# Adding exp(-m) to the softmax denominators on TensorE, and taking a batch's token maxima later, in a fused attention and soft-MoE kernel

## The chip, the core and the metric

The kernel runs on one core of a Trainium2 chip. A core has a matrix engine (TensorE, PE in the profile; its weight loads are PEld), a vector engine (VectorE, DVE), a scalar engine (ScalarE, ACT), GpSimd (POOL) and SyncE (SP). Each works through its own instructions in order, and they wait for one another by semaphores. POOL and SP also issue DMAs here. PE writes to PSUM, which DVE and ACT read; POOL works in SBUF.

The metric is the device time of one launch in microseconds. Three runs of the kernel before took 297.56, 299.50 and 299.66 us; the median is 299.5.

## The reference

For each of 8 batches and 12 heads, with 448 tokens and 64 features per head, it computes attention with a softmax whose denominator has one more term, exp(-m):

```
scores = scale * q @ k.T
m = max(scores, -1);  e = exp(scores - m)
attn = e / (sum(e, -1) + exp(-m) + 1e-09)
out = attn @ v
```

The output, 3584 tokens by 768, goes into a soft mixture of experts with 8 experts of 4 slots each:

```
logits = x @ phi                            # 3584 x 32
d = softmax over tokens;   slot_input = d.T @ x
slot_out[e] = relu(slot_input[e] @ w1[e]) @ w2[e]
c = softmax over slots;    result = c @ slot_out
```

Both softmaxes subtract a maximum first: the one for c the maximum of each token (over the 32 slots), the one for d the maximum of each slot (over the tokens).

## The kernel before

**Pairs and slots.** Heads are taken in 48 pairs, six pairs to a batch. The main loop (L758) runs over slots s, one pair each, in two half-slots y = 0 and 1; the order of every engine's work is written out by hand. In its slot a pair has its transposed scores computed on PE (`Bk`: a score product, L367, and a product that subtracts the maximum, L370, both into ps_b buffers of a pool of four), then exponentials on ACT (L372, L402). Between these stand the score products of a later pair (`A`, L285, into ps_a buffers of a pool of three), whose row maxima DVE takes (L287; L307 for the last 64 tokens). PE also transposes q and k of the pair six slots ahead (`T`, L256; copied by ACT at L263 or by DVE at L265).

**Denominators.** The product of the exponentials with v (`AV`, L436) has a column of ones beside the 64 columns of v, so column 64 of each of its seven tiles of 65 columns is the sum of the exponentials. All seven lie in one PSUM bank, of which there is one. Key blocks i = 0 and 1 are multiplied in the pair's own slot, i = 2 and 3 in the first half of the next one, followed by the eight products of the last 64 queries. Then `N1` copies the bank into ubuf on ACT (L449), and `N2` adds exp(-m) and 1e-9 on DVE (L464), takes the reciprocal (L465) and scales on POOL (L469, L479, L480) into x. `PX` transposes x on PE (L501) and ACT casts it (L507).

**exp(-m).** Every third slot a group of three pairs has its maxima prepared: `W1` on POOL (L318, L314), `W2` on PE (L336, L337), `W3` on ACT: a cast (L342), and two exponentials (L345, L348) that write ec, three pairs by seven columns in f32. There are 17 groups.

**A batch's part of the experts.** The list `post` spreads a batch's steps over half-slots of the following pairs. The first makes the logits on PE (`l_mm`, L535, into ps_l), copies them to l in SBUF on ACT (`l_ev`, L558) and takes the token maxima on DVE (`c_max`, L562). Half a slot later PE transposes l (`l_turn`, L570, with the f32 identity identf) and DVE takes maxima over it (L572), and POOL subtracts the token maxima (`c_sub`, L577). `s_max` (L582, L583), `d_sub` (L591), the exponentials (L596, L601), `s_mm` (L623), `s_add` (L632) and `c_turn` (L627, L628) follow. The last batch has an order of its own. After the loop the experts and the result are computed.

POOL's queue also issues the loads of q, k, v and of the expert weights between its other work, SP's the weights staged in memory and the output.

Of the kernel before, what the change touches and what calls it, by code (L numbers as in the profile page):

```python
# [10 lines left out]
AX = mybir.AxisListType  # L11
AF = mybir.ActivationFunctionType
ALU = mybir.AluOpType
# [13 lines left out]
W65 = 65  # L27
# [4 lines left out]
def kernel(  # L32
# [10 lines left out]
    nc = tc.nc  # L43
    B, H, S, D = q.shape
# [5 lines left out]
    KC = DD // 128  # L50
# [3 lines left out]
    NPAIR = B * PB  # L54
# [14 lines left out]
    identf = const.tile([128, 128], F32, name="identf")  # L69
# [87 lines left out]
    with ExitStack() as at:  # L157
# [73 lines left out]
        mx, ngm, ec, mT, eT, av, us = {}, {}, {}, {}, {}, {}, {}  # L231
# [39 lines left out]
        group = {n: (m, n - a) for m, (a, z) in enumerate(zip(firsts, firsts[1:] + [NPAIR])) for n in range(a, z)}  # L271
        mg, mpl = (lambda n: group[n][0]), (lambda m: (0, (firsts + [NPAIR])[m + 1] - firsts[m]))
# [67 lines left out]
        def W3(g):  # L340
            t = psm.tile([128, S], BF16, tag="mT", name="mT")
            nc.scalar.copy(t, st["ps_m"][:, 0:S])  # L342
            mT[g] = t
            e = psm.tile([128, NP, 7], F32, tag="ec", name="ec", bufs=3)
            nc.scalar.activation(e[:, :, 0:6].rearrange("p l (i h) -> p i l h", i=3),  # L345
                                 ngm[g][:, 0:18].rearrange("p (i l h) -> p i l h", i=3, h=2),
                                 AF.Exp, scale=scale)
            nc.scalar.activation(e[:, :, 6], ngm[g][:, 18:21], AF.Exp, scale=scale)  # L348
            ec[g] = e


# [63 lines left out]
        def av_tile(n):  # L415

            if n >= NPAIR - 3:
                return psA.tile([128, 512], F32, tag="a", name="ps_av")
            return psV.tile([128, 512], F32, tag="v", name="ps_av")

        def AV(n, i, qs):
            g, pl = divmod(n, NP)
            if i == 0 and qs[0] == 0:
                av[n] = av_tile(n)
            a = av[n]
            if n == NPAIR - 1 and i == 0 and qs[0] == 3:
                av_half["ps"] = psA.tile([128, 512], F32, tag="a", name="ps_av")
            for u in qs:
                for hl in range(2):
                    if u < 3:  # L430
                        c0 = (2 * u + hl) * W65
                        o, qc = a[:, c0:c0 + W65], slice(u * 128, (u + 1) * 128)
                    else:
                        t, z = (av_half["ps"], 0) if n == NPAIR - 1 else (a, 6 * W65)
                        o, qc = t[64 - 64 * hl:128 - 64 * hl, z:z + W65], slice(384, 448)
                    nc.tensor.matmul(o, eT[n, i, hl][:, qc], vp[g % 2][:, 2 * pl + hl, i, 0:W65],  # L436
                                     start=(i == 0 and u == 0 and hl == 0) or (u == 3 and i == 0 and n == NPAIR - 1),
                                     stop=(i == 3), skip_group_check=True)

        av_half = {}  # L440
        on_pool = lambda n: n < NPAIR - 4
# [10 lines left out]
        def N2(n):  # L452
            g, pl = divmod(n, NP)
            b, pb = divmod(n, PB)
            u = us[n]
            eng = nc.gpsimd if on_pool(n) else nc.vector
            rec = psm.tile([128, 7], F32, tag="rec", name="rec", bufs=3)
            e = ec[mg(n)][:, group[n][1], :]
            if n == NPAIR - 1:
                nc.vector.scalar_tensor_tensor(rec[:, 6:7], av_half["ps"][:, D:W65], 1e-9, e[:, 6:7],  # L460
                                               op0=ALU.add, op1=ALU.add)
                nc.vector.scalar_tensor_tensor(rec[:, 0:6], u[:, 0:6, D], 1e-9, e[:, 0:6], op0=ALU.add, op1=ALU.add)
            else:
                nc.vector.scalar_tensor_tensor(rec, u[:, :, D], 1e-9, e, op0=ALU.add, op1=ALU.add)  # L464
            nc.vector.reciprocal(rec, rec)  # L465
            x = xb[b % 2]
            c = pb * 128
            rec2 = psm.tile([128, 2], F32, tag="rec2", name="rec2", bufs=3)
            eng.tensor_mul(  # L469
                x[:, 0:3, c:c + 128].rearrange("p i (h d) -> p i h d", h=2),  # L470
                u[:, 0:6, 0:D].rearrange("p (i h) d -> p i h d", h=2),
                rec[:, 0:6].rearrange("p (i h) -> p i h", h=2).unsqueeze(3).to_broadcast([128, 3, 2, D]))
            if n == NPAIR - 1:

                for h in range(2):
                    r = slice(64 - 64 * h, 128 - 64 * h)
                    nc.scalar.mul(x[r, 3, c + 64 * h:c + 64 * h + 64], av_half["ps"][r, 0:D], rec[r, 6:7])
                return
            eng.tensor_scalar(rec2, halfm, rec[:, 6:7], None, op0=ALU.mult)  # L479
            eng.tensor_mul(  # L480
                x[:, 3, c:c + 128].rearrange("p (h d) -> p h d", h=2),
                u[:, 6, 0:D].unsqueeze(1).to_broadcast([128, 2, D]),
                rec2.unsqueeze(2).to_broadcast([128, 2, D]))
# [32 lines left out]
        def P(b):  # L516
            l, new = lb[b % 2], lb[(b + 1) % 2][:, 4, :]
            eng = nc.gpsimd if b < B - 2 else nc.vector
            x = xb[b % 2]
            v = {}  # L520
# [3 lines left out]
            def l_mm(js):  # L524
                if js[0] == 0:
                    if b < B - 1:
                        v["ps_l"] = pa([128, 4, NS], F32, "ps_l")
                    else:
                        t = psV.tile([128, 512], F32, tag="v", name="ps_l")
                        v["ps_l"] = t[:, 0:4 * NS].rearrange("p (i s) -> p i s", i=4)  # L530
                        v["ps_lT"] = t[:, 4 * NS:4 * NS + 129]

                def plain(j, tiles=range(4)):
                    for i in tiles:
                        nc.tensor.matmul(v["ps_l"][:, i, :], xT(b, j)[:, i * 128:(i + 1) * 128], phi_sb[:, j, :],  # L535
                                         start=(j == 0 and i == 0), stop=(j == KC - 1), skip_group_check=True)

                for j in js:
                    if b < B - 1 or j == 0:
                        plain(j)  # L540
                    if b == B - 1 and j == 3:
                        nc.tensor.matmul(v["ps_lT"][:, 128:129], flat(old),
                                         ident[:, 0:1], start=False, stop=True, skip_group_check=True)
                    if b == B - 1:

                        for i in range(4):
                            nc.tensor.matmul(v["ps_lT"][NS * i:NS * i + NS, 0:128], phi_sb[:, j, :],
                                             xT(b, j)[:, i * 128:(i + 1) * 128],
                                             start=False, stop=(j == KC - 1), skip_group_check=True)
                        if j == KC - 1:  # L550
                            l_turn()
                            keep_busy(2)
                            s_max()
                        if j:
                            plain(j)
# [3 lines left out]

            def c_max():  # L560
                m = psm.tile([128, 4], F32, tag="cm", name="cm")
                nc.vector.reduce_max(m, v["ps_l"] if b < B - 1 else l[:, 0:4, :], axis=AX.X)  # L562
                v["cm"] = m

            def l_turn():
                if b == B - 1:
                    ps = v["ps_lT"]
                else:
                    ps = pa([128, 128], F32, "ps_lT")
                    nc.tensor.transpose(ps, flat(l[:, 0:4, :]), identf)  # L570
                m = psm.tile([128, 1], BF16, tag="sm", name="sm")
                nc.vector.reduce_max(m, ps, axis=AX.X)  # L572
                v["sm"] = m
                v["z"] = psm.tile([128, 9, NS], F32, tag="z", name="z", bufs=1)
# [75 lines left out]

            both = lambda *fs: (lambda: [f() for f in fs])
            if b < B - 1:
                return [both(lambda: l_mm(range(KC)), l_ev, c_max), both(l_turn, c_sub), both(s_max, d_sub),
                        both(exps, corr)] + ([c_turn, both(s_mm, s_add)] if late(b) else [both(s_mm, s_add), c_turn])
            return [lambda: l_mm([0]), lambda: l_mm([1]), lambda: l_mm([2]), lambda: l_mm([3]), lambda: l_mm([4]),
                    both(lambda: l_mm([PB - 1]), l_ev,
# [34 lines left out]
        ps = psV.tile([128, 512], F32, tag="v", name="ps_idle")  # L691
# [255 lines left out]
        for half in range(2):  # L947
            for bp in range(B // 2):
                o = (half * (B // 2) + bp) * 4
                nc.tensor.matmul(ps_cs[:, o:o + 4], cT[:, bp, half, :, :].rearrange("p b j -> p (b j)"), band,  # L950
                                 start=True, stop=True)
# [80 lines left out]
```

## Time and profile before

| what | value |
|---|---|
| median of 3 runs | 299.5 us |
| span of the profiled execution | 299.0 us |
| granted PE clock, mean | 0.956 (1.00 until 270 us) |
| main loop | about 33 to 250 us |
| busy in the stretch 120 to 140 us | PE 19.96, ACT 19.08, DVE 19.48, POOL 16.60 of 20 us |
| busy from 260 to 270 us | PE 9.71, DVE 3.82, ACT 4.02, POOL 0.00 of 10 us |

What lies around the span of the profiled execution is taken as the difference to the median, 0.5 us. In the rows below, a group of instructions has its line, engine, operation, output and inputs, shape and count, then busy time and the mean duration of one in ns, then the engine's idle time before them and what ended it. In an answer in order of time the columns are start and duration in us, engine, line, operation, tiles, shape and count; in brackets stands the idle time before it and what released it. A matmul's duration holds its passage through the array, and the next can start long before its end, so how fast PE goes is read from the starts. A row of a stretch has its length, then busy us and counts of PE, PEld, DVE, ACT and POOL, then granted clock, DMA share and GB/s.

### The profile page before, as it was taken

The numbers are of one execution on the slowest core, as the hardware profiler recorded it, in microseconds if no ns is written. First come the engines' busy times: TensorE is split into PE (matmuls) and PEld (weight loads), VectorE is DVE, ScalarE is ACT, GpSimd is POOL, SyncE is SP. The second block draws the span as 40 slices with busy tenths as digits, with TensorE's granted clock in tenths as the row PEclk, the third lists the DMA queues.
The fourth block names the chain that finished last, engine by engine and source line by source line (L and its number), as shares of the span: only waits on it lengthen the run. The fifth ranks groups of instructions, "written<-read, shape, count | busy, mean of one in ns | idle before, by whom it ended". The sixth has DMA issues, their size and how long they took to land.

```text
span 299.0 us, 12398 instructions
## 1 busy us (share of the span) xinstructions
PE 271.4 (91%) x5174; PEld 162.5 (54%) x5174; DVE 249.7 (84%) x581; ACT 249.8 (84%) x559; POOL 195.9 (66%) x391
## 2 busy tenths in 40 slices
PE   5999899999999999999899999999999999996820
PEld 4445456566666566566556666656665555652100
DVE  5899799999999989999889999998999675537930
ACT  3569999999899989998989899989999987337820
POOL 8792887979696979887879697978686633000000
PEclk9999999999999999999999999999999999997555
DMA  7999998999999999999999999999799989908997
GB/s 132 147 143 208 149 138 138 188 165 188 185 204 179 184 176 202 163 182 182 202 159 184 176 199 152 196 183 196 125 150 187 213 185 263 344 10 318 380 453 322
DMA packets 47015, 58.67 MB, mean 196 GB/s; under 512 B 2800, under 2 KB 39920, under 8 KB 46704
## 3 DMA queue, kind: packets, MB, share of 16 engines
q0 software_dynamic: 40304, 42.29, 89.6%
q1 hardware_dynamic: 6656, 15.60, 13.8%
q8 instruction: 40, 0.66, 0.8%
q14 instruction: 15, 0.12, 0.1%
HBM read 89.16 MB, written 15.14 MB: 349 GB/s over the span
## 4 chain that ended last, share of the span: by engine, by line
PE 68%; ACT 10%; DVE 6%; POOL 6%; issue 4%; DMA 2%; DVEq 0%; POOLq 0%; ACTq 0%
PE ps_av L436 15%; PE ps_a L285 10%; PE ps_b L367 7%; PE ps_b L370 7%; PE ps_t L256 5%; PE ps_b L396 5%; PE ps_x L501 3%; PE ps_b L399 3%; ACT W L402 2%; PE ps_o L925 2%; DVE mx L298 2%; PE ps_s L623 2%; PE ps_h L862 2%; PE ps_so L882 2%; ACT W L263 2%
## 5 line engine op out<-in xcount | busy, mean ns | idle before, releaser
L287 DVE TENSOR_REDUCE mx<-ps_a 128x1 f32<-128x448 f32 x250 | 137.3, 613 | 4.6 <-PE ps_a L285 3.5
L372 ACT ACTIVATE W<-ps_b 128x448 bf16<-128x448 f32 x250 | 120.4, 574 | 0.0
L285 PE MATMUL ps_a<-W 64*128 64x448 bf16 x250 | 80.9, 352 | 0.0
L367 PE MATMUL ps_b<-W 64*128 64x448 bf16 x250 | 70.5, 352 | 1.1
L436 PE MATMUL ps_av<-W 128*128 128x65 bf16 (+1 forms) x1536 | 64.9, 196 | 2.2 <-issue 1.6
L436 PEld LDWEIGHTS <-W 128*128 128x128 bf16 (+1 forms) x1536 | 50.5, 100 | 30.2 <-issue 26.4
L370 PE MATMUL ps_b<-mT,sel 64*128 64x448 bf16 x250 | 66.5, 350 | 0.0
L469 POOL TENSOR_TENSOR W<-ubuf,rec 128x384 bf16<-128x384 f32 x44 | 36.3, 824 | 35.7 <-ACT W L507 19.3
L402 ACT ACTIVATE W<-ps_b 128x448 bf16<-128x448 f32 x86 | 46.1, 574 | 2.0 <-PE ps_b L399 2.0
L256 PEld LDWEIGHTS <-W 64*64 64x64 bf16 x1344 | 29.3, 112 | 12.7 <-issue 4.3
L507 ACT CAST W<-ps_x 128x512 bf16<-128x512 f32 x47 | 28.6, 608 | 7.4 <-PE ps_x L501 7.2
L256 PE MATMUL ps_t<-ident,W 64*64 64x64 bf16 x1330 | 30.6, 195 | 2.4 <-ACT W L215 1.4
L307 DVE TENSOR_REDUCE mx<-ps_a 128x1 f32<-128x448 f32 x48 | 29.5, 615 | 1.4 <-PE ps_a L304 1.4
L285 PEld LDWEIGHTS <-W 64*128 64x128 bf16 x250 | 23.4, 94 | 9.8
L114 POOL DMA_DIRECT2D W<-in_moe_w_dram x30 | 22.6, 755 | 7.9 <-PE ps_b L399 7.8
L370 PEld LDWEIGHTS <-sel 64*128 64x128 bf16 x250 | 19.6, 94 | 14.4 <-issue 5.6
L396 PE MATMUL ps_b<-W 64*64 64x448 bf16 (+1 forms) x134 | 27.1, 374 | 0.3
L449 ACT COPY ubuf<-ps_av 128x455 f32<-128x455 f32 x44 | 25.1, 571 | 0.8 <-POOL W L408 0.6
L399 PE MATMUL ps_b<-mT,sel 64*64 64x448 bf16 (+1 forms) x134 | 25.1, 354 | 0.1
L263 ACT COPY W<-ps_t 128x896 bf16<-128x896 bf16 x21 | 19.5, 927 | 6.5 <-PE ps_t L256 6.5
L298 DVE TENSOR_REDUCE mx<-ps_a 128x1 f32<-128x448 f32 x38 | 21.1, 616 | 1.9 <-PE ps_a L294 1.9
L480 POOL TENSOR_TENSOR W<-ubuf,rec 128x128 bf16<-128x128 f32 x44 | 17.5, 398 | 3.7
(156 smaller groups left out, 446.6 us busy)
## 6 DMA issues: line engine op xcount, KB each, us to landing
W<-in_moe_w_dram POOLq DMA_DIRECT2D x24, 768.0 KB, 9.9
W<-in_v_dram POOLq DMA_DIRECT2D x32, 192.0 KB, 6.5
out_dram<-W SPq DMA_DIRECT2D x2, 2688.0 KB, 10.0
W<-in_q_dram POOLq DMA_DIRECT2D x15, 336.0 KB, 6.3
W<-in_k_dram POOLq DMA_DIRECT2D x15, 336.0 KB, 7.5
stage<-in_moe_w_dram POOLq DMA_DIRECT2D x4, 768.0 KB, 9.6
W<-stage SPq DMA_DIRECT2D x4, 576.0 KB, 7.3
out_dram<-W SPq DMA_DIRECT2D x6, 384.0 KB, 3.0
```

The costliest lines, as they stand in the source:

```text
L256: nc.tensor.transpose(o, src[r, pl, tok * D:(tok + 1) * D], ident[r, r])
L285: nc.tensor.matmul(ps[:, 0:S], t[r, 0, i * 128:(i + 1) * 128], t[r, 1, :], start=True, stop=True)
L287: nc.vector.reduce_max(m[:, c:c + 1], ps[:, 0:S], axis=AX.X)
L307: nc.vector.reduce_max(mx[g][:, c:c + 1], ps[:, 0:S], axis=AX.X)
L367: nc.tensor.matmul(pss[hl][:, 0:S], t[rs[hl], 1, cols], t[rs[hl], 0, :], start=True, stop=False)
L370: nc.tensor.matmul(pss[hl][:, 0:S], sel[rs[hl], 2 * pl + hl:2 * pl + hl + 1].to_broadcast([64, 128]), mT[mg(n)][rs[hl], :], start=False, s ...
L372: nc.scalar.activation(e[:, hl, :], pss[hl][:, 0:S], AF.Exp, scale=scale)
L396: nc.tensor.matmul(outs[hl], t[rs[hl], 1, cols], t[rs[hl], 0, :], start=True, stop=False)
L399: nc.tensor.matmul(outs[hl], sel[rs[hl], 2 * pl + hl:2 * pl + hl + 1].to_broadcast([64, m]), mT[mg(n)][rs[hl], :], start=False, stop=True)
L402: nc.scalar.activation(e, p[:, 0:S], AF.Exp, scale=scale)
L436: nc.tensor.matmul(o, eT[n, i, hl][:, qc], vp[g % 2][:, 2 * pl + hl, i, 0:W65], start=(i == 0 and u == 0 and hl == 0) or (u == 3 and i == ...
L469: eng.tensor_mul(x[:, 0:3, c:c + 128].rearrange("p i (h d) -> p i h d", h=2), u[:, 0:6, 0:D].rearrange("p (i h) d -> p i h d", h=2), rec[: ...
```

## The change

There are two edits.

The first moves the sum of the denominators to PE. POOL adds 1e-9 to ec once for each group. After the products of key block i = 3 PE multiplies the f32 identity by the seven f32 columns of the pair's ec and accumulates them onto column 64 of the seven tiles in PSUM. The copy in ubuf then holds the whole denominator, and DVE only takes the reciprocal. The last pair keeps its sums on DVE.

The second lets `c_max` of all batches but the last read the copy l in SBUF in place of ps_l, and issues it half a slot later, after the transposition of l and ahead of the maxima over it.

```diff
             nc.scalar.activation(e[:, :, 6], ngm[g][:, 18:21], AF.Exp, scale=scale)
+            nc.gpsimd.tensor_scalar(e, e, 1e-9, None, op0=ALU.add)
             ec[g] = e
...
+            if i == 3 and qs[0] == 0 and n < NPAIR - 1:
+
+                nc.tensor.matmul(a[:, 0:7 * W65].rearrange("p (s c) -> p s c", c=W65)[:, :, D], identf,
+                                 ec[mg(n)][:, group[n][1], :], start=False, stop=True, skip_group_check=True)
...
             if n == NPAIR - 1:
-                nc.vector.scalar_tensor_tensor(rec[:, 6:7], av_half["ps"][:, D:W65], 1e-9, e[:, 6:7],
-                                               op0=ALU.add, op1=ALU.add)
-                nc.vector.scalar_tensor_tensor(rec[:, 0:6], u[:, 0:6, D], 1e-9, e[:, 0:6], op0=ALU.add, op1=ALU.add)
-            else:
-                nc.vector.scalar_tensor_tensor(rec, u[:, :, D], 1e-9, e, op0=ALU.add, op1=ALU.add)
-            nc.vector.reciprocal(rec, rec)
+                nc.vector.tensor_add(rec[:, 6:7], av_half["ps"][:, D:W65], e[:, 6:7])
+                nc.vector.tensor_add(rec[:, 0:6], u[:, 0:6, D], e[:, 0:6])
+            nc.vector.reciprocal(rec, rec if n == NPAIR - 1 else u[:, :, D])
...
                 m = psm.tile([128, 4], F32, tag="cm", name="cm")
-                nc.vector.reduce_max(m, v["ps_l"] if b < B - 1 else l[:, 0:4, :], axis=AX.X)
+                nc.vector.reduce_max(m, l[:, 0:4, :], axis=AX.X)
                 v["cm"] = m
...
                     nc.tensor.transpose(ps, flat(l[:, 0:4, :]), identf)
+                    c_max()
                 m = psm.tile([128, 1], BF16, tag="sm", name="sm")
...
-                return [both(lambda: l_mm(range(KC)), l_ev, c_max), both(l_turn, c_sub), both(s_max, d_sub),
+                return [both(lambda: l_mm(range(KC)), l_ev), both(l_turn, c_sub), both(s_max, d_sub),
```

## The prediction

> **What bounds the kernel now.** I read the page's busy shares and chain first, then the busy times by stretch, the instructions in order of time on PE, DVE and ACT over two slots, and last the groups by line and shape.
>
> ```profile
> PE 271.4 (91%) x5174; PEld 162.5 (54%) x5174; DVE 249.7 (84%) x581; ACT 249.8 (84%) x559; POOL 195.9 (66%) x391
> ...
> PE 68%; ACT 10%; DVE 6%; POOL 6%; issue 4%; DMA 2%; DVEq 0%; POOLq 0%; ACTq 0%
> ```
>
> The chain is mostly PE, but that share hides short stalls, because a matmul's recorded time is longer than its step in the stream. The stretch of one batch (six slots, one pair of heads each) says more:
>
> ```profile
> 90.43:120.05 29.62, 28.85 (x593) 18.20 (x592) 27.81 (x66) 28.08 (x67) 24.58 (x47) 1.00 1.15 184
> ```
>
> Of 29.62 us PE is busy 28.85, ACT 28.08 and DVE 27.81: three engines within 4% of one another, at a granted clock of 1.00. So the question is which of them sets each slot, and that is seen in start-to-start times. Slot A (from 110.02) and the first half of slot B (from 114.51) on PE:
>
> ```profile
> 110.61 0.53 PE L367 MATMUL ps_b<-W 64*128 64x448 bf16 x2
> 110.79 0.54 PE L370 MATMUL ps_b<-mT,sel 64*128 64x448 bf16 x2
> 111.21 0.35 PE L285 MATMUL ps_a<-W 64*128 64x448 bf16 x1
> ```
> ```profile
> 115.12 0.84 PE L367 MATMUL ps_b<-W 64*128 64x448 bf16 x2
> 115.62 0.53 PE L370 MATMUL ps_b<-mT,sel 64*128 64x448 bf16 x2
> ```
>
> Two row-tiled products step on after 0.18 to 0.20 us where nothing holds them. Before 111.21 the step is 0.42, a stall of 0.23; before 115.62 it is 0.50, a stall of 0.31. The first waits for a ps_a buffer, so for DVE:
>
> ```profile
> 109.97 0.39 DVE L632 TENSOR_TENSOR acc<-acc,ps_s 128x224 f32<-128x224 f32 x1 [0.28 <-PE ps_s L623]
> 110.27 0.16 DVE L464 SCALAR_TENSOR_TENSOR rec<-ubuf,ec 128x7 f32<-128x7 f32 x1
> 110.46 0.20 DVE L465 RECIPROCAL rec<-rec 128x7 f32<-128x7 f32 x1
> 110.58 2.17 DVE L287 TENSOR_REDUCE mx<-ps_a 128x1 f32<-128x448 f32 x4
> ```
>
> The second waits for a ps_b buffer, so for ACT, which has run without a pause since 110.13:
>
> ```profile
> 110.13 0.59 ACT L507 CAST W<-ps_x 128x512 bf16<-128x512 f32 x1 [0.95 <-PE ps_x L501]
> 110.62 1.85 ACT L372 ACTIVATE W<-ps_b 128x448 bf16<-128x448 f32 x4
> 112.36 0.54 ACT L449 COPY ubuf<-ps_av 128x455 f32<-128x455 f32 x1
> ...
> 114.15 0.92 ACT L263 COPY W<-ps_t 128x896 bf16<-128x896 bf16 x1
> 114.93 0.63 ACT L507 CAST W<-ps_x 128x512 bf16<-128x512 f32 x1
> ```
>
> Read in the same way, the six slots of a batch stall PE for A 0.23 (DVE), B 0.34 (ACT), C (from 120.05) 0.13 and 0.14 (DVE), D (124.65) 0.20 (ACT), E (129.19) 0.16 (ACT) and 0.12 (DVE), F (133.92) 0.05 and 0.07 (DVE). That is about 1.4 us per batch, 0.7 of it DVE's. From the cast of mT in slot B to the last exponential of F, ACT runs almost without a pause.
>
> **The parts of the change and their cost.**
>
> ```profile
> L314 POOL TENSOR_SCALAR ngm<-mx 128x21 bf16<-128x21 f32 x15 | 4.2, 280 | 0.0
> L464 DVE SCALAR_TENSOR_TENSOR rec<-ubuf,ec 128x7 f32<-128x7 f32 x47 | 7.7, 163 | 0.1
> L562 DVE TENSOR_REDUCE cm<-ps_l 128x4 f32<-128x128 f32 x7 | 2.0, 292 | 2.6 <-ACT lb L558 2.6
> L570 PE MATMUL ps_lT<-identf,lb 128*128 128x128 f32 x7 | 2.1, 304 | 0.0
> L570 PEld LDWEIGHTS ps_lT<-identf,lb 128*128 128x128 f32 x7 | 1.0, 142 | 0.0
> L950 PE MATMUL ps_cs<-band,cT 128*128 128x4 bf16 x8 | 0.3, 165 | 0.0
> ```
>
> *Removed: 47 sums on DVE (L464).* From L464's start to L465's is 0.19 us (110.27 to 110.46), so 47 x 0.19 = 8.9 us of DVE go. The last pair keeps two DVE sums in place of two; nothing changes there.
>
> *Added: 47 products of identf (128x128, f32) with 7 columns, on PE, in the first half of a slot.* The trace has no such product. From below: the eight 4-column bf16 products of L950, each with its own 128x128 load, start 0.025 us apart (0.34 us for all, the last one recorded at 0.165). From above: load and product of L570 fully exposed, 0.143 + 0.305 = 0.45. The nearest row is L570, which also puts a 128x128 f32 operand into the array: 0.14 us on PE from its start to the next matmul's, in the chain and in the stream. I take X = 0.14; it reaches below where only 7 columns stream, and above where one product needs several such steps.
>
> That L570 may be cheaper than a product is what the Trainium skill says ("TensorE: Matmul & The Clock Gate", Terms: transpose mode is four times faster for FP32). By that rule a product would cost up to four of L570's steps, 0.56 us, as an estimate; no run here shows one.
>
> *Where X is hidden.* I go through a batch and ask what ends each stretch. (1) A's start to B's stall: ACT ends it. X lies beside ACT's row of work, but L449 (112.36) waits for the end of the slot's AV products and has no slack of its own; without L464 PE arrives 0.19 earlier there, so X up to 0.2 costs nothing, above that X - 0.2. (2) B's stall to the cast of mT: PE ends it (ACT waits for ps_m 0.07), the cost is X. (3) C to D's stall: as (1). (4) D's stall to E's: ACT ends it, X - 0.16 when positive. (5) E's stall to the next A: PE ends it (L507 waits 0.95 for PE). Two products are paid, 2X, and DVE's stalls of 0.12, 0.05 and 0.07 go: 2X - 0.24. With X = 0.14: 0 + 0.14 + 0 + 0 + 0.04 = 0.18 per batch. The 41 regular slots are 6.8 batches: +1.3 us. Seven products lie in the ramp and the last slots, where PE often waits anyway; half of 7 x 0.14 makes +0.5.
>
> *Added: 17 sums on POOL (e + 1e-9).* 0.28 us each by L314, 4.8 us on an engine busy 24.6 of 29.6. Each waits for the second exponential on ACT. Behind it on POOL stand c_sub (L577), the scaling of x (L469) and, after these, the DMA issues of the slot. In the slot after B, POOL stood idle 1.45 us before L469 (until 120.75); the exponential ends at 120.17, the sum would end at 120.45, L577 at 120.87. L469 is 0.1 us late, and POOL's next pauses (0.75 us before L176 at 93.45) take that up: 0. The first product that needs the sum comes two half-slots later, some 6 us. If that cover were gone, 17 x 0.1 is 1.7 us at most.
>
> *Moved: seven maxima (L562).* It now reads the copy l, behind the transposition, past two L287, an L307 and where DVE has it the L265; no DMA and no queue of SP moves with it. DVE loses a wait of 2.6/7 = 0.37 us in mid-slot B and gets 0.21 (L562's step) back at its end. Both sides: a gain of 0.37 per batch if DVE set that stretch, a loss of 0.21 where it delays C's first reductions. DVE reaches C about 0.3 earlier by PE's measure (0.37 + 0.19 - 0.21), so C's two stalls of 0.27 go; but D's stall, ACT's, takes the place of what they gave. I take 0. The new wait, c_sub for the maximum, has until the exponentials in D (127.12).
>
> The sum: 299.0 (span) + 1.3 + 0.5 = 300.8, and the 0.5 us by which the median of the runs (299.5) stands over the span: **301.3 us**, no change that can be told. A measurement here tells about 1%, 3 us, from none.
>
> **Rivals.**
>
> *Two steps per product (slower).* If the array takes a 32-bit operand in parts, X is two of L570's steps, 0.28. Then ACT covers no longer: 0.28 + (0.56 - 0.24) + 2 x 0.08 + 0.12 = 0.88 per batch, 6.0 us, and 1.0 for the seven others: 306.5. It decides from X = 0.2 on. For it: f32 loads are recorded at 142 ns, bf16 ones at 97. Against it: with 7 columns, less than L570's stream of 128 has to pass. The Trainium skill ("FP8 and Floating Point Precision", TensorE Precision Notes) says true FP32 takes four passes; with L950's 0.025 plus the 0.045 of longer load for each, that estimate is also 0.28. At the upper bound of 0.45 the same sum gives 1.9 per batch, 13.0 + 1.6: 314.
>
> *DVE's relief shows (faster).* If DVE's lateness is behind ACT's too, its 0.74 us of stalls per batch are all gained, 5.0 us, against 47 products. At X = 0.07 these cost 3.3: 297.8; at 0.025 they cost 1.2: 295.7. Against it: ACT's row without pauses in A, and in C to F.
>
> *The change does nothing on the path.* X near 0.07 gives 3X - 0.24 = -0.03 per batch: 299.5.
>
> **How the numbers follow.** X = 0.14 or somewhat less, with ACT as cover: 0.55 (the last rival's 0.10 within it). Two steps: 0.27; the upper bound: 0.05; relief: 0.13. The range leaves out the upper bound, the cheapest relief and a tail of each: 297 to 307.5. Faster by over 1% (below 296.5) is a third of the relief case and little else: 0.06. Slower (above 302.5) is all of the two-step and upper cases and a sixth of the forecast's, whose 1.8 us can grow by half with five odd stalls of 0.5 to 1.3 us per execution: 0.41. The same: 0.53.
>
> **What would show it.** In the changed profile: the step from the product to the next AV matmul is X. DVE's busy time falls by some 8 us. PE's stalls in A, C and F's first halves go; those in B and D stay, or grow. L562 has no wait for L558. Wrong would be: X above 0.2; POOL's sum seen as the releaser of PE, or W1 late behind it; ACT idle in C to F, which would mean that DVE had set the pace.

## The result and the profile after

The changed kernel takes **306.06 us** (median of four runs, 305.66 to 307.08) against 298.84 us of the kernel before: a ratio of **1.0245**, 95% interval 1.0208 to 1.0283. It is slower by 2.4%, where no change was forecast; the time is almost that of the rival with two steps per product (306.5).

First the page of the changed kernel, its busy times, and the same stretch as before (from the start of slot C to the start of the next one).

```profile
PE 277.2 (91%) x5268; PEld 173.3 (57%) x5268; DVE 244.6 (80%) x534; ACT 253.5 (83%) x559; POOL 201.1 (66%) x408
```
```profile
92.01:122.41 30.40, 29.71 (x607) 19.64 (x605) 27.14 (x60) 28.70 (x67) 25.17 (x49) 1.00 1.13 178
```

PE has 94 more matmuls, not 47, and DVE 47 instructions fewer and 5.1 us less work (some 8 were forecast; the maxima of L287 are recorded 2.9 us longer in all, 140.2 in place of 137.3). Per batch DVE falls from 27.81 to 27.14 us, PE rises from 28.85 to 29.71, and the batch is 30.40 long. The groups by line and shape name the new work.

```profile
L442 PE MATMUL ps_av<-ec,identf 128*128 128x7 f32 x94 | 17.0, 253 | 0.0
L442 PEld LDWEIGHTS ps_av<-ec,identf 128*128 128x128 f32 x94 | 14.2, 191 | 0.0
L349 POOL TENSOR_SCALAR ec<-ec 128x21 f32<-128x21 f32 x17 | 4.7, 276 | 18.6 <-ACT ec L348 18.5
```

Each f32 product is two loads and two products, with loads recorded at 191 ns. What it costs PE is read from the starts in slot A, in order of time:

```profile
112.83 0.54 PE L371 MATMUL ps_b<-mT,sel 64*128 64x448 bf16 x2
113.14 0.35 PE L285 MATMUL ps_a<-W 64*128 64x448 bf16 x1
113.42 0.53 PE L437 MATMUL ps_av<-W 128*128 128x65 bf16 x12
113.78 0.37 PE L442 MATMUL ps_av<-ec,identf 128*128 128x7 f32 x2
114.08 0.32 PE L437 MATMUL ps_av<-W 128*64 128x65 bf16 x8
114.33 0.36 PE L285 MATMUL ps_a<-W 64*128 64x448 bf16 x1
```

From the first AV product to the next score product is 0.91 us (113.42 to 114.33); before it was 0.72 (111.48 to 112.20). So X is about 0.20 here, as in all slots but two: 0.21 in C, and 0.22 in B, where the products of the logits follow. The prediction wanted X to be read from the step between the product and the next AV product. That step is 0.30, but some 0.10 us of it stood at this place before, where the AV products change their shape. The stall ahead of the last score product (the step to 113.14) is 0.31 in place of 0.42: DVE's relief, but 0.11 us, not 0.19.

The first halves of slots B and D, from the same view:

```profile
117.25 0.84 PE L368 MATMUL ps_b<-W 64*128 64x448 bf16 x2
117.75 0.53 PE L371 MATMUL ps_b<-mT,sel 64*128 64x448 bf16 x2
...
127.68 0.84 PE L368 MATMUL ps_b<-W 64*128 64x448 bf16 x2
128.18 0.53 PE L371 MATMUL ps_b<-mT,sel 64*128 64x448 bf16 x2
```

B's step of 0.50 is unchanged. D, which stalled by 0.20 before, now has the same step of 0.50, a stall of 0.31 (0.34 with the step ahead of it). ACT's row in slot C in order of time tells why, first in the kernel before, then in the changed one:

```profile
120.67 1.85 ACT L372 ACTIVATE W<-ps_b 128x448 bf16<-128x448 f32 x4
122.39 0.57 ACT L449 COPY ubuf<-ps_av 128x455 f32<-128x455 f32 x1
```
```profile
123.03 1.86 ACT L373 ACTIVATE W<-ps_b 128x448 bf16<-128x448 f32 x4
124.93 0.54 ACT L454 COPY ubuf<-ps_av 128x455 f32<-128x455 f32 x1
...
126.70 0.93 ACT L263 COPY W<-ps_t 128x896 bf16<-128x896 bf16 x1
127.49 0.63 ACT L509 CAST W<-ps_x 128x512 bf16<-128x512 f32 x1
```

Before, the copy of ps_av started as soon as the four exponentials let ACT go, 1.72 us after the first of them. Now it starts 1.90 us after it: ACT waits some 0.19 us for the AV products, which end behind the new product. From there ACT runs without a pause to the cast at 127.49, for which slot D waits. In slot A the copy waited for the AV products before, too, and it now starts 2.43 us after the slot's start in place of 2.34 (114.49 from 112.06, before 112.36 from 110.02). So the product stands ahead of ACT's row of work, not beside it.

The table adds up a batch. A slot is taken from PE's first score product after a ps_x group to the next such; each entry is the median over the regular batches, in us.

| kernel | time | ratio to before (95%) | A | B | C | D | E | F | batch |
|---|---|---|---|---|---|---|---|---|---|
| before, first profile | 298.84 | | 4.50 | 5.55 | 4.59 | 4.54 | 4.74 | 5.07 | 28.99 |
| changed | 306.06 | 1.0245 (1.0208 to 1.0283) | 4.58 | 5.77 | 4.66 | 4.88 | 4.77 | 5.28 | 29.93 |
| first edit alone | 305.62 | 1.0254 (1.0195 to 1.0313) | 4.58 | 5.76 | 4.65 | 4.87 | 4.77 | 5.28 | 29.91 |
| second edit alone | 301.23 | 1.0117 (1.0050 to 1.0183) | 4.48 | 5.54 | 5.02 | 4.53 | 4.74 | 5.08 | 29.40 |
| no sum | 297.74 | 0.9964 (0.9937 to 0.9991) | 4.37 | 5.60 | 4.58 | 4.55 | 4.62 | 5.09 | 28.81 |
| product of zeros | 307.23 | 1.0288 (1.0234 to 1.0343) | 4.69 | 5.76 | 4.66 | 4.87 | 4.94 | 5.28 | 30.20 |
| bf16 product | 301.17 | 1.0088 (1.0053 to 1.0122) | 4.38 | 5.62 | 4.59 | 4.56 | 4.73 | 5.09 | 28.96 |

The 0.94 us per batch make 6.4 us over 6.8 batches, and the four slots after these are 0.16 to 0.22 us longer each, 0.8: 7.2 us, the difference of the medians. The two profiles differ by 5.0 us only, because the first profile of before holds 3.5 us of odd long slots (what single slots take beyond the median of their letter) and that of the changed kernel 0.6. Outside the slots the two differ as well: the first regular slot starts 0.7 us earlier in the changed kernel, and the output's DMA ends 1.4 us later behind the last computation. Neither is part of the 7.2 us, and neither is explained.

### The profile page after: what moved, and what is told of

Same layout as the page of the kernel before. It is cut to its first block, busy times and chain, and to the rows that moved or that the text cites. A ratio compares the mean times of both kernels' runs of the same rounds, so it can differ in the third digit from the quotient of the medians.

```text
span 304.0 us, 12519 instructions
## 1 busy us (share of the span) xinstructions
PE 277.2 (91%) x5268; PEld 173.3 (57%) x5268; DVE 244.6 (80%) x534; ACT 253.5 (83%) x559; POOL 201.1 (66%) x408
## 4 chain that ended last, share of the span: by engine, by line
PE 70%; ACT 12%; DVE 4%; DMA 3%; issue 3%; POOL 3%; DVEq 0%; POOLq 0%; ACTq 0%
PE ps_av L437 15%; PE ps_a L285 9%; PE ps_b L368 7%; PE ps_b L371 7%; PE ps_b L397 5%; PE ps_t L256 5%; ACT W L263 3%; ACT W L403 3%; PE ps_av L442 3%; DVE mx L298 3%; PE ps_x L503 2%; ACT W L509 2%; PE ps_b L400 2%; DMA W<-in_k_dram 2%; PE ps_o L928 2%
## 5 line engine op out<-in xcount | busy, mean ns | idle before, releaser
L287 DVE TENSOR_REDUCE mx<-ps_a 128x1 f32<-128x448 f32 x250 | 140.2, 617 | 17.2 <-PE ps_a L285 14.3
L373 ACT ACTIVATE W<-ps_b 128x448 bf16<-128x448 f32 x250 | 119.6, 568 | 0.0
L437 PE MATMUL ps_av<-W 128*128 128x65 bf16 (+1 forms) x1536 | 66.9, 196 | 0.6 <-ACT ubuf L454 0.5
L403 ACT ACTIVATE W<-ps_b 128x448 bf16<-128x448 f32 x86 | 45.2, 565 | 2.9 <-PE ps_b L400 2.9
L307 DVE TENSOR_REDUCE mx<-ps_a 128x1 f32<-128x448 f32 x48 | 29.6, 616 | 0.6 <-PE ps_a L304 0.6
L371 PEld LDWEIGHTS <-sel 64*128 64x128 bf16 x250 | 19.5, 94 | 14.4 <-issue 5.2
L454 ACT COPY ubuf<-ps_av 128x455 f32<-128x455 f32 x44 | 24.3, 553 | 0.7 <-issue 0.2
L298 DVE TENSOR_REDUCE mx<-ps_a 128x1 f32<-128x448 f32 x38 | 21.2, 620 | 2.1 <-PE ps_a L294 1.9
```

What stands on the lines that cost most here:

```text
L287: nc.vector.reduce_max(m[:, c:c + 1], ps[:, 0:S], axis=AX.X)
L371: nc.tensor.matmul(pss[hl][:, 0:S], sel[rs[hl], 2 * pl + hl:2 * pl + hl + 1].to_broadcast([64, 128]), mT[mg(n)][rs[hl], :], start=False, s ...
L373: nc.scalar.activation(e[:, hl, :], pss[hl][:, 0:S], AF.Exp, scale=scale)
L403: nc.scalar.activation(e, p[:, 0:S], AF.Exp, scale=scale)
```

## The experiments

**One edit at a time.** The first edit alone keeps the token maxima where they were:

```diff
-                nc.vector.reduce_max(m, l[:, 0:4, :], axis=AX.X)
+                nc.vector.reduce_max(m, v["ps_l"] if b < B - 1 else l[:, 0:4, :], axis=AX.X)
...
-                    c_max()
```

> The first edit alone: the sum on PE and POOL, the token maxima as in the kernel before. Theory 1 (the f32 product steps PE by 0.20 to 0.22 us and nearly all 47 are paid): 305 to 306.5 us, slot D still about 0.3 longer than before. Theory 2 (the later maxima push work into slot D): 303 to 304 us, slot D near 4.75.

305.62 us, and the same six slots as the changed kernel within 0.01 us, slot D's 4.87 among them. The later maxima are not the cause of the loss. That is theory 1.

The second edit alone:

> The second edit alone: the token maxima half a slot later from the copy, the sums on DVE. Theory 1: 298.5 to 299.5 us, no change; if the 0.14 us stall in the second half of slot C goes, slot D's grows by as much. Theory 2: 1 to 2 us slower, slot D over 4.8.

301.23 us, and slot C, not D, is the longer one: 5.02 in place of 4.59. Neither theory had this place. DVE and POOL at C's start, in order of time:

```profile
121.53 0.28 DVE L562 TENSOR_REDUCE cm<-lb 128x4 f32<-128x128 f32 x1
121.72 0.28 DVE L573 TENSOR_REDUCE sm<-ps_lT 128x1 bf16<-128x128 f32 x1
121.92 0.39 DVE L464 SCALAR_TENSOR_TENSOR rec<-ubuf,ec 128x7 f32<-128x7 f32 x1
122.35 0.20 DVE L465 RECIPROCAL rec<-rec 128x7 f32<-128x7 f32 x1
122.46 0.57 DVE L287 TENSOR_REDUCE mx<-ps_a 128x1 f32<-128x448 f32 x1
```
```profile
121.89 0.39 POOL L578 TENSOR_TENSOR z<-lb,cm 128x128 f32<-128x128 f32 x1 [1.52 <-DVE cm L562]
```

The maxima now end just ahead of the sum L464, and c_sub on POOL, which waited for them, runs at the same moment. The sum takes 0.39 us in place of its median of 0.157. It does so all six times that c_sub runs beside it (392 to 398 ns), and each time it ends 21 to 26 ns behind c_sub. Where only DMA issues run on POOL beside it, it takes 152 to 168 ns. The 0.19 us step of the maxima and some 0.24 us of the longer sum are the 0.43 us by which C grows. In the changed kernel the sum is gone from DVE, and C is 4.66.

**DVE's relief by itself.**

```diff
-            else:
-                nc.vector.scalar_tensor_tensor(rec, u[:, :, D], 1e-9, e, op0=ALU.add, op1=ALU.add)
-            nc.vector.reciprocal(rec, rec)
+            nc.vector.reciprocal(rec, rec if n == NPAIR - 1 else u[:, :, D])
```

> The kernel before without the sum of the 47 denominators on DVE; exp(-m) and 1e-9 are left out of them, and nothing takes their place. It prices the relief of DVE alone. Theory 1 (ACT and the ps_a buffers hold what DVE gives up): 297 to 298.5 us, 1 to 2 us less. Rival (DVE sets the pace): about 294 us, 0.7 us per batch less.

297.74 us, a ratio of 0.9964 (0.9937 to 0.9991): about 1 us. Slots A and E gain 0.11 to 0.13 us each, the others nothing (B is 0.05 longer), though DVE has 0.19 us less to do in each. That refutes the rival in which DVE sets the pace. Slot A in this kernel, in order of time:

```profile
110.44 0.36 PE L285 MATMUL ps_a<-W 64*128 64x448 bf16 x1
...
111.21 0.53 PE L370 MATMUL ps_b<-mT,sel 64*128 64x448 bf16 x2
111.51 0.35 PE L285 MATMUL ps_a<-W 64*128 64x448 bf16 x1
```
```profile
110.69 0.20 DVE L463 RECIPROCAL rec<-ubuf 128x7 f32<-128x7 f32 x1
110.83 0.62 DVE L287 TENSOR_REDUCE mx<-ps_a 128x1 f32<-128x448 f32 x1
```

The step to 111.51 is still 0.30. DVE takes up the first maximum at 110.83, 0.39 us after its product started (0.36 recorded for the product), and ends it 0.62 us later, at 111.46; PE's fourth ps_a product starts at 111.51. With three ps_a buffers that product has to wait for this first one: some 1.07 us after the slot's start, however early DVE is free. That is a floor, and 0.11 of the 0.23 us that I had read as DVE's lateness belong to it. Slot F of the same kernel (from 105.36) shows the floor with a DVE that is not late at all:

```profile
105.76 1.16 DVE L287 TENSOR_REDUCE mx<-ps_a 128x1 f32<-128x448 f32 x2 [0.60 <-PE ps_b L367]
```
```profile
106.44 0.35 PE L285 MATMUL ps_a<-W 64*128 64x448 bf16 x1
```

DVE has stood idle for 0.60 us when it takes up the first maximum, again 0.40 us after the slot's start, and the fourth product still starts 1.08 us after it.

**The same with four ps_a and three ps_b buffers**, to test that floor.

```diff
-        psA = pool("psA", 3, space=PSUM)
-        psB = pool("psB", 4, space=PSUM)
+        psA = pool("psA", 4, space=PSUM)
+        psB = pool("psB", 3, space=PSUM)
```

> The kernel before without the 47 sums on DVE (exp(-m) and 1e-9 left out of them, as in the run that prices DVE's relief), and with four ps_a and three ps_b buffers in place of three and four. It asks what holds the 0.12 us stall that stays in slot A when DVE has been relieved. If it is the ring of three ps_a buffers, the step before the second group's last score product falls from 0.30 to 0.19 us; if it is DVE's lateness, it stays. The steps that wait for ps_b get longer, so the time may well be up: 297 to 306 us.

320.36 us, in one run. The step in question is 0.20 us, as the ring of buffers asks. But a step before it that waits for ps_b has grown to 0.45 us, so PE comes to the product 0.43 us later than it did, and DVE's lateness would have been used up too. The run doesn't tell the two apart; the floor rests on the start times above, on slot F's above all.

**The product by itself.** Seven columns of zeros at the same place; DVE keeps its sums.

```diff
+            if i == 3 and qs[0] == 0 and n < NPAIR - 1:
+                nc.tensor.matmul(a[:, 0:7 * W65].rearrange("p (s c) -> p s c", c=W65)[:, :, D], identf,
+                                 zero7, start=False, stop=True, skip_group_check=True)
```

> The kernel before with one more f32 product per pair at the same place, of seven columns of zeros: it adds nothing to the sums, which stay on DVE, and POOL has no new work. It prices the product by itself. Theory 1 (a step of 0.20 to 0.22 us on PE, of which only some 0.2 per batch is covered): about 1.0 us per batch, 305.5 to 307 us. Rival (the price is POOL's sum and its wait): under 302 us.

307.23 us. A batch takes 30.20 us, 1.21 more than before: six products at 0.20. All is paid. Against this kernel the changed one is 0.27 us per batch better (A 0.11, E 0.17): what DVE's relief brings beside the product.

**POOL's sum.**

```diff
-            nc.gpsimd.tensor_scalar(e, e, 1e-9, None, op0=ALU.add)
```

> The changed kernel without POOL's 17 sums of 1e-9, which are left out of 47 denominators. Theory 1: 305 to 306.5 us, as the changed kernel. Rival (POOL's wait for ACT costs): 303 to 304 us.

305.97 us against 306.06: nothing. POOL's wait for ACT (18.5 us in all, in the groups above) stands where POOL waited before for other things (L469's waits fell from 35.7 to 16.0 us).

**The kernel before, profiled again.**

> The kernel before once more, for a second profile of it. The six slots of a batch again sum to 28.9 to 29.0 us; the odd long slots (3.5 us in the first profile) differ, and the span is 296 to 298 us if they are fewer.

A span of 297.5 us and 28.98 us per batch; the odd slots make 1.8 us in place of 3.5. This execution took 299.25 us, 1.75 more than its span, and the profiled one of the changed kernel 305.81 with a span of 304.0. About 1.8 us lie around a span, not the 0.5 that I had taken.

**A 16-bit product.**

```diff
-            nc.gpsimd.tensor_scalar(e, e, 1e-9, None, op0=ALU.add)
+            eb = psm.tile([128, NP, 7], BF16, tag="eb", name="eb", bufs=3)
+            nc.gpsimd.tensor_scalar(eb, e, 1e-9, None, op0=ALU.add)
...
-                nc.tensor.matmul(a[:, 0:7 * W65].rearrange("p (s c) -> p s c", c=W65)[:, :, D], identf,
-                                 ec[mg(n)][:, group[n][1], :], start=False, stop=True, skip_group_check=True)
+                nc.tensor.matmul(a[:, 0:7 * W65].rearrange("p (s c) -> p s c", c=W65)[:, :, D], ident,
+                                 ecb[mg(n)][:, group[n][1], :], start=False, stop=True, skip_group_check=True)
```

> The changed kernel with a bf16 product: POOL writes e + 1e-9 as bf16, and the bf16 identity multiplies it. All else is as in the changed kernel. Theory 1 (the f32 product is the cost): one load and a step of 0.03 to 0.05 us, 298 to 300 us. Theory 2 (the sum on POOL, its wait for ACT, or the later maxima are the cost): 304 us or more.

Its groups by line and shape show one product per pair:

```profile
L445 PE MATMUL ps_av<-eb,ident 128*128 128x7 bf16 x47 | 8.0, 170 | 0.0
```

The slots are those of the kernel without any sum, within 0.02 us (E apart, which in three of its six takes 0.2 us or more over the 4.62 of the others): the price of the product is gone. The time is 301.17 us all the same, above the forecast of 298 to 300. What follows the regular slots takes 77.4 us of the span in place of 75.2 and 75.6 in the two profiles of before. 0.45 us of it is one pause among the products of the first expert layer, and 1.7 to 2.1 us is the time from the last engine's work to the end of the output's DMA (14.4 us in place of 12.3 and 12.7); the work on the result between these two is 0.3 us shorter. Whether the later maxima have a part in it was asked with the maxima as before, beside the 16-bit product:

```diff
-                nc.vector.reduce_max(m, l[:, 0:4, :], axis=AX.X)
+                nc.vector.reduce_max(m, v["ps_l"] if b < B - 1 else l[:, 0:4, :], axis=AX.X)
```

> The bf16 product with the maxima as in the kernel before. If the later maxima cost nothing beside the sums on PE (as the first edit alone suggests), 300 to 301.5 us like the bf16 product; if they are what keeps it above the kernel before, 297.5 to 298.5 us.

300.60 us, and 77.3 us after the slots: the later maxima have no part that shows.

**A copy moved from ACT to DVE in slot A.**

```diff
-            elif first or n % 6 in (1, 3):
+            elif first or n % 6 == 3:
```

> The changed kernel with the copy of q and k in slot A (every sixth) on DVE in place of ACT. If ACT's row from slot A on sets the stall of 0.34 us in slot B, that falls to about 0.12 and a batch gains 0.15 to 0.2 us: 304.5 to 305 us. If PE's products alone set these slots, it stays at 306.

304.40 us, a ratio to before of 1.0202 (1.0187 to 1.0217), and 0.25 us per batch less (29.68), all of it in slot B, whose step of 0.50 falls to 0.19:

```profile
117.33 0.53 PE L368 MATMUL ps_b<-W 64*128 64x448 bf16 x2
117.52 0.54 PE L371 MATMUL ps_b<-mT,sel 64*128 64x448 bf16 x2
117.83 0.35 PE L285 MATMUL ps_a<-W 64*128 64x448 bf16 x1
```

So ACT's row from slot A on did set that stall; what is left is the floor ahead of the fourth score product (0.31).

The same line changed in the kernel with the bf16 product and the later maxima:

> The same copy on DVE with the bf16 product: 28.7 us per batch or less by theory 1, 1 to 2 us under the kernel before in the loop; 299 to 300 us if the end of the kernel stays 2 us longer, as in the two other runs with a bf16 product, 297 to 298 us if not.

28.75 us per batch, and the regular slots end 3.1 us earlier than in the second profile of before (218.86 against 221.91); 1.4 us of these are odd slots, and 0.7 an earlier start. What follows takes 77.35 us. The time is 299.25 us, a ratio of 1.0037 (1.0016 to 1.0058): no version here that computes the whole denominator beats the kernel before.

## Why the prediction was wrong

*X.* This is the first term that was mis-sized: 0.14 by L570's step, 0.20 to 0.22 measured. The row was of one load and one product; an f32 product is two of each. "Two steps" was the rival's mechanism, and 94 matmuls for 47 products show it; only its 0.28 was too much. X above 0.2 was among the signs that I had named for being wrong.

By the Trainium skill ("FP8 and Floating Point Precision", TensorE Precision Notes) true FP32 takes four passes. The trace agrees that there are several, and records two; whether each holds two passes no run here shows.

*The cover.* With X = 0.21 my own sum would have given 0.21 + (0.42 - 0.24) + 0.02 + 0.05 = 0.46 us per batch; 0.94 was measured. The rest is the step "X lies beside ACT's row of work" in stretches (1) and (3), and DVE's stalls, which I let go in stretch (5).

(1) I let PE arrive at A's AV products 0.19 us earlier by DVE's relief; it was 0.11, since the rest of the stall is the ring of three buffers. A grew by 0.08 to 0.10 in place of 0.01. (3) C grew by 0.07, and D's stall by 0.14: 0.21 in place of 0.01, the whole of X. The copy of ps_av in C waits for the product, so ACT's row starts later, and slot D pays. That C grew by no more than 0.07 is no relief of DVE. Its first stall of 0.13 is the floor and stayed. Its second, of 0.14, went because PE comes to it later: it stayed in the kernel without a sum (C 4.58) and went with the product of zeros (C 4.66), where DVE has all its work. (5) I had taken 0.24 us of DVE's stalls off the price of E's and F's products, 0.18 in all. They didn't go. F's 0.12 stayed in the kernel without a sum, too (F 5.09), so it was not DVE's. E's 0.12 was DVE's (E fell to 4.62 there), but now that E no longer waits for ACT at its start, the floor takes its place. So both products were paid, 0.40.

Stretches (2) and (4) came as forecast: B grew by 0.22, X itself, and D's product less E's stall of 0.16, which went, leaves 0.04 where I had 0.05.

*What held.* DVE's relief brings little (1 us alone, with nothing in its place). POOL's sum costs nothing, nor do the later maxima beside it; their gain of up to 0.37 was rightly taken as 0. That the maxima alone would cost 2.6 us I had not seen: I counted their 0.21 us at C's start, not what POOL would do to the sum behind them. B's stall stayed, and D's grew. Of the three stalls that were to go, those in the first halves of A, C and F, only A's went, and that by half.

*The base.* I took the profiled execution for a usual one and put 0.5 us around its span. It was a long one (3.5 us of odd slots), and 1.8 us lie around a span; the two errors nearly cancel. (0.18 us in 6.8 batches make 1.2, not 1.3, which changes nothing.) What the odd slots wait for was not settled.

*The sign.* No change was the likeliest case by a sum whose cost and cover were both taken at the good end. At the X of the rival, 0.28, my sum gave 0.88 per batch and 306.5 us; it met the time with a price that was too high and a cover that was too wide, so that the two errors cancelled: luck, not a right account.

## What to carry to other kernels

Where PE, ACT and DVE are all busy over 90%, taking work from one of them gains only the stalls that it alone sets. So read for each stall when its releaser could have started: a ring of buffers stalls PE by the latency of one product and one reduction even when the engine behind it is free. An instruction put into PE's queue ahead of products whose result ACT copies is not beside ACT's work, it is in front of it. A small product in f32 is not small: with 7 columns it moved PE's stream by 0.20 to 0.22 us, and in bf16, with the term rounded to 16 bits, it was nearly free. Whether the two loads or the two products make this price was not separated; no run changed the number of columns.

## What the runs showed of the hardware

An f32 product of 7 columns is issued as two loads (191 ns recorded, 142 for the f32 transposition, 97 for bf16) and two products, and moves the stream of PE by 0.20 to 0.22 us; with bf16 operands, as one load and one product, by about 0.01 to 0.03.

A DVE sum of 128x7 with two operands in SBUF took 0.39 us in place of 0.157 while POOL subtracted two SBUF operands, and ended 21 to 26 ns after POOL's instruction. The Trainium skill ("SBUF — State Buffer", Who interferes with whom) says that a DVE instruction with two SBUF inputs contends with a GpSimd instruction that reads SBUF; the trace agrees, with these numbers.

With three PSUM buffers for products that DVE reduces, the fourth product started 1.07 us after the first at the earliest: 0.40 us to the start of the reduction, 0.62 for the reduction, and 0.05 to the product, with DVE idle for 0.60 us beforehand or not.

The end of the kernel, mostly the output's DMA, differs between the kernels with the same code there. From the last computation to the end of the span it takes 12.3 to 12.9 us in the four profiles without the product and with the buffers as before, 13.1 to 13.7 in the five with the f32 product, and 14.4 in the three with the bf16 product, a profile each. Its cause stays open.
